# Warming matmuls on a ready-made constant, and the softmax's head masks copied by VectorE

## The chip, the cores and the metric

The kernel runs on one core of a Trainium2 chip. The metric is the device time of one execution in microseconds (us); a lower time is better. Every kernel here was timed in several runs, in turns with the kernel before on the same chip, so each comparison below has its own runs of before.

## The reference, cut to what matters

A causal convolution of 7 taps per head (the taps are a softmax over `weight`), then two matrix products with an ELU between them:

```python
w = softmax(weight, axis=-1)                       # 8 heads x 7 taps
out = einsum('hk,bskhg->bshg', w, unfold(x))       # x: 8 x 4096 x 192, padded by 6 in front
h = out.reshape(32768, 192) @ w_in                 # 192 x 2048
g = where(h > 0, h, exp(minimum(h, 0)) - 1)
return g @ w_out                                   # 2048 x 192, float32
```

## The kernel before: the parts that the change and the argument touch

The work is cut into 32 tiles of 1024 tokens. In the steady state each hidden block of 128 x 512 passes through four engines: TensorE multiplies (line 1029), ScalarE takes the exponential into `E` (760), GpSimd clamps it (714), VectorE makes the product `gT` (871), and TensorE multiplies again (1052). The convolution of all tiles but the first is a matmul with a band matrix `Tm` (1004), which is made from the taps by way of a buffer in DRAM.

The start-up differs: the first tile is loaded by itself (`xs`), cast, transposed on TensorE and convolved tap by tap. Meanwhile GpSimd makes an identity and two masks, and then issues the loads of weights and of the later tiles:

```python
@block.gpsimd
    g.memset(ones[:], 1.0).then_inc(s_id)
    g.affine_select(out=ident[:], in_=ones[:], ...).then_inc(s_id)
    for step in range(2):                          # owner: which head owns which partition
        W(s_id, 2 + step)
        g.affine_select(out=owner[:, :], ...).then_inc(s_id)
    W(s_id, 4)
    g.affine_select(out=block8[:, :, :], ...).then_inc(s_id)
    load_w_in(0); load_w_in(1); load_w_out(0)
    for gr in range(2): load_x(1, gr)
    load_w_out(1); load_w_out(2)
    for gr in range(2): load_x(2, gr)
    for i, (n, u) in enumerate(units):             # the clamps
        ...                                        # (cut: a first load of tile 3 here)
        W(s_exp, i + 1)
        g.tensor_scalar(out=E[...], in0=E[...], scalar1=1.0, scalar2=0.0, op0=min, op1=max)

@block.vector
    v.memset(zw[:], 0.0).then_inc(s_zw)            # operand of the warming matmuls
    v.memset(wband[:], 0.0).then_inc(s_wb)
    v.memset(xbh[:, :, :, :], 0.0).then_inc(s_xz)
    ...                                            # softmax, then (cut)
    W(s_id, 5)
    v.tensor_tensor(wnb[:], block8[:], ..., mult)

@block.tensor
    W(s_zw, 1)
    for _ in range(item[2]):                       # WARM = (6, 1, 4): six, softmax, four
        pe.matmul(H[:, bank, :], zw[:, 0:P], zw[:, 0:GS], start=True, stop=True)
```

## Time and profile before

| | before |
|---|---|
| median of the first three runs | 718.77 us (718.75 to 719.13) |
| span of the profiled run | 716.6 us |
| TensorE, ScalarE, GpSimd, VectorE busy | 99%, 95%, 93%, 90% |
| first hidden matmul, first exponential, first clamp | 10.55, 11.39, 12.86 us |
| start of TensorE's last group (224 matmuls) | 704.35 us |

TensorE bounds the kernel from about 45 us on, and the change alters nothing there. So one asks when the steady state begins. In all lines below, the first number is the start in us from the span's start and the second the length.

### The profile page before, as it was taken

The page shows a single profiled execution, that of the slowest core. Times are in us where ns is not written, and L with a number is a line of the kernel's source. Part 1 is how long each engine was busy: PE and PEld are TensorE (multiplying, and loading weights), DVE is VectorE, ACT ScalarE, POOL GpSimd, SP SyncE. Part 2 cuts the span into 40 slices and gives each one's busy share as a digit, 9 for nine tenths or more (in the row PEclk, how much of TensorE's full clock was granted, in tenths as well). Part 3 has the DMA queues.
Part 4 walks back from the last instruction along what each step waited for, and adds up shares of the span by engine and source line. Part 5 has one row for each costly group of instructions (what it writes and reads, how often), then busy time and mean ns, then how long its engine had stood idle before and what let it go on. Part 6 is the DMA issues. An engine that isn't in the chain of part 4 may idle for free.

```text
span 716.6 us, 27662 instructions
## 1 busy us (share of the span) xinstructions
PE 710.7 (99%) x11873; PEld 681.6 (95%) x11873; DVE 641.5 (90%) x1049; ACT 677.4 (95%) x1290; POOL 663.6 (93%) x1112
## 2 busy tenths in 40 slices
PE   8999999999999999999999999999999999999998
PEld 4699999999999999999999999999999999999998
DVE  7999889998898998899998999988989988999994
ACT  6999999999999999999999999999999999999994
POOL 9999999999999999999999999999999999999893
PEclk9999999999999999999999999999999999999999
DMA  9635334564433544444554344544445534444212
GB/s 183 99 72 95 65 73 78 93 86 76 80 79 74 95 89 64 80 85 79 87 91 69 73 76 95 87 73 76 85 73 91 93 63 78 87 80 83 63 43 69
DMA packets 132303, 58.80 MB, mean 82 GB/s; under 512 B 98374, under 2 KB 131412, under 8 KB 132180
## 3 DMA queue, kind: packets, MB, share of 16 engines
q0 software_dynamic: 43504, 16.77, 22.4%
q1 hardware_dynamic: 88388, 39.37, 22.0%
q8 instruction: 93, 1.52, 0.9%
q10 hardware_dynamic: 288, 0.88, 0.4%
q14 instruction: 30, 0.25, 0.1%
HBM read 34.63 MB, written 25.46 MB: 84 GB/s over the span
## 4 chain that ended last, share of the span: by engine, by line
PE 96%; POOL 2%; ACT 1%; DVE 0%; issue 0%; DVEq 0%; POOLq 0%
PE H L1052 54%; PE H L1029 37%; PE H L1004 4%; POOL xg L631 1%; ACT E L760 1%; POOL E L714 1%; POOL w_in L651 0%; POOL w_out L662 0%; DVE gT L871 0%; ACT csb L756 0%; POOL owner L679 0%; DVE osb L862 0%; POOL block L689 0%; POOL ident L668 0%; POOL ones L666 0%
## 5 line engine op out<-in xcount | busy, mean ns | idle before, releaser
L871 DVE SCALAR_TENSOR_TENSOR gT<-E,H 128x512 f16<-128x512 f32 x1024 | 631.8, 681 | 62.8 <-POOL E L714 58.4
L1029 PE MATMUL H<-att,w_in 64*128 64x512 bf16 x3072 | 679.8, 376 | 1.2 <-DVE gT L871 0.9
L1052 PE MATMUL H<-w_out,gT 64*128 64x192 f16 x8192 | 680.4, 243 | 0.1
L714 POOL TENSOR_SCALAR E<-E 128x512 f32<-128x512 f32 x1024 | 603.0, 611 | 41.1 <-ACT E L760 34.2
L1052 PEld LDWEIGHTS H<-w_out,gT 64*128 64x128 f16 x8192 | 606.7, 94 | 17.5 <-PE H L1052 1.5
L760 ACT ACTIVATE E<-H 128x512 f32<-128x512 f32 x1024 | 585.0, 601 | 23.9 <-PE H L1029 0.4
L1029 PEld LDWEIGHTS H<-att,w_in 64*128 64x128 bf16 x3072 | 275.3, 93 | 7.8 <-DVE gT L871 2.9
L1004 PE MATMUL H<-xg,Tm 64*128 64x240 bf16 x496 | 90.9, 263 | 0.0
L756 ACT ACTIVATE csb<-H 112x480 bf16<-112x480 f32 x124 | 70.7, 570 | 0.4 <-PE H L1004 0.3
L767 ACT ACTIVATE osb<-H 128x384 f32<-128x384 f32 (+1 forms) x129 | 62.0, 482 | 6.9 <-PE H L1052 6.8
L631 POOL DMA_DIRECT2D xg<-in_x_dram x62 | 54.7, 884 | 0.2 <-issue 0.2
L1004 PEld LDWEIGHTS H<-xg,Tm 64*128 64x128 bf16 x496 | 42.6, 94 | 1.2 <-DVE gT L871 0.3
L862 DVE COPY osb<-H 128x192 f32<-128x192 f32 x1 | 0.4, 357 | 7.3 <-PE H L1052 7.3
L909 PE MATMUL H<-zw 128*128 128x512 bf16 x10 | 4.3, 588 | 1.2 <-DVE zw L775 1.2
L909 PEld LDWEIGHTS H<-zw 128*128 128x128 bf16 x10 | 1.2, 134 | 3.0 <-issue 1.7
L651 POOL DMA_DIRECT2D w_in<-in_moe_w_in_dram x6 | 3.6, 612 | 0.0
L736 ACT ACTIVATE xb<-xs 128x512 bf16<-128x512 f32 x2 | 1.2, 622 | 2.4 <-DMA xs<-in_x_dram 2.4
L978 PE MATMUL H<-xT,taps 64*64 64x256 bf16 (+1 forms) x50 | 2.6, 317 | 0.0
L662 POOL DMA_DIRECT2D w_out<-in_moe_w_out_dram x3 | 2.5, 853 | 0.0
L978 PEld LDWEIGHTS H<-xT,taps 64*64 64x64 bf16 x50 | 2.0, 106 | 0.5 <-issue 0.2
L729 ACT ACT_TABLE_LOAD x1 | 1.3, 1283 | 1.2 <-PEq L1119 1.2
L936 PEld LDWEIGHTS H<-ident,xb 64*64 64x64 bf16 x48 | 1.2, 126 | 0.8 <-ACT xb L736 0.8
(45 smaller groups left out, 20.5 us busy)
## 6 DMA issues: line engine op xcount, KB each, us to landing
out_dram<-osb SPq DMA_DIRECT2D x126, 192.0 KB, 2.9
xg<-in_x_dram POOLq DMA_DIRECT2D x61, 240.0 KB, 4.5
xs<-in_x_dram ACTq DMA_DIRECT2D x1, 768.0 KB, 4.6
w_in<-in_moe_w_in_dram POOLq DMA_DIRECT2D x6, 128.0 KB, 4.7
att<-csb SPq DMA_TRANSPOSE x31, 3.9
w_out<-in_moe_w_out_dram POOLq DMA_DIRECT2D x2, 192.0 KB, 7.9
w_out<-in_moe_w_out_dram POOLq DMA_DIRECT2D x1, 384.0 KB, 11.8
w_in<-w_in SPq DMA_DIRECT2D x1, 336.0 KB, 6.8
```

The source lines that it names most:

```text
L631: g.dma_start(xg[0:rows, b, 2 * w0 + gr : 2 * w1 : 2, :], src).then_inc(s_x[b][gr], 16)
L651: g.dma_start(w_in[0:HP, j, c0:c1], bass.AP(tensor=moe_w_in.tensor, offset=8 * j * FF + c0, ap=[[CPH * FF, HEADS], [FF, 8], [1, c1 - c0]], ...
L714: g.tensor_scalar(out=E[:, i % NE, :], in0=E[:, i % NE, :], scalar1=1.0, scalar2=0.0, op0=ALU.min, op1=ALU.max,).then_inc(s_clp)
L756: a.activation(*conv_evac(W, m), ACT.Copy).then_inc(s_ce)
L760: a.activation(E[:, i % NE, :], H[:, bank_of[item], :], ACT.Exp).then_inc(s_exp)
L767: a.activation(*out_evac(W, *item[1:]), ACT.Copy).then_inc(s_oev[item[2]])
L871: v.scalar_tensor_tensor(out=gT[:, s % NG3, q, u, :], in0=E[:, i % NE, :], scalar=1.0, in1=H[:, bank_of[item], :], op0=ALU.subtract, op1=A ...
L909: pe.matmul(H[:, bank, :], zw[:, 0:P], zw[:, 0:GS], start=True, stop=True)
L978: ins = pe.matmul(H[to, bank_of["d", j] + (j == 2 and c0 > 0), c0:c1], taps[rows, tap, rows], xT[rows, j, HALO - PAD + tap + c0 : HALO - P ...
L1004: ins = pe.matmul(H[:, bank_of["c", m], 256 * q : 256 * q + UC], Tm[rows, h, :], xg[rows, s % NXB, :, CPH * h : CPH * (h + 1)].rearrange(" ...
L1029: ins = pe.matmul(H[:, bank_of[item[:3]], :], w_in[HP * r : HP * (r + 1), j, FC * q : FC * (q + 1)], att[HP * r : HP * (r + 1), s % 2, j, ...
L1052: ins = pe.matmul(acc_of(k, g)[:, D * kb : D * (kb + 1)], gT[HP * rt : HP * (rt + 1), t % NG3, q, g, t0 : t0 + P], w_out[HP * rt : HP * (r ...
```

## The change

Its intent is to start the warming of TensorE earlier (it no longer waits for a memset), and to free GpSimd of three selects, so that its loads are issued earlier.

```diff
-WARM = (6, 1, 4)
+WARM = (8, 1, 4)
@@ gpsimd
-            for step in range(2):
-                W(s_id, 2 + step)
-                g.affine_select(out=owner[:, :], ...)
-            W(s_id, 4)
-            g.affine_select(out=block8[:, :, :], ...)
             load_w_in(0)
@@ vector
-            v.memset(zw[:], 0.0).then_inc(s_zw)
             v.memset(wband[:], 0.0).then_inc(s_wb)
             v.memset(xbh[:, :, :, :], 0.0).then_inc(s_xz)
+            W(s_id, 2)
+            v.tensor_copy(owner[:, :]..., ident[0:HEADS, 0:HEADS]...).then_inc(s_own)
+            v.tensor_copy(block8[:, :, :], ident[0:HEADS, 0:HEADS]...).then_inc(s_own)
@@ tensor
-                    W(s_zw, 1)
-                        pe.matmul(H[:, bank, :], zw[:, 0:P], zw[:, 0:GS], ...)
+                        pe.matmul(H[:, bank, :], const 1.0 as (P, P), const 1.0 as (P, GS), ...)
-                    W(s_id, 4)          # ahead of the softmax's matmul
+                    W(s_id, 2)
```

(Cut: the declarations of `zw`, `s_zw`, `s_own`, a wait of the loads on `s_zw`, and VectorE's wait for the masks, now on `s_own`.)

More of the change, by code (lines that the diff above doesn't have):

```diff
@@ L455, in bass_lightweight_conv__then__act_elu_kernel @@
         wband = sbuf("wband", [P, HEADS + 1, BW], BF16)
-        zw = sbuf("zw", [P, GS], BF16)
         scr = sbuf("scr", [P, 2], FP32)
@@ L468, in bass_lightweight_conv__then__act_elu_kernel @@
         s_id = sema("s_id")
+        s_own = sema("s_own")
         s_xs = sema("s_xs")
@@ L480, in bass_lightweight_conv__then__act_elu_kernel @@
         s_z = sema("s_z")
-        s_zw = sema("s_zw")
         s_h = sema("s_h")
@@ L622, in load_x @@
                     W(s_cv, CU * (s - NXB))
-                if s == NXB:
-                    W(s_zw, 1)
                 def windows(w0, w1, rows):
@@ L675, in _gpsimd @@
                 channel_multiplier=1,
-            ).then_inc(s_id)
-            for step in range(2):
-                W(s_id, 2 + step)
-                g.affine_select(
-                    out=owner[:, :],
-                    in_=owner[:, :] if step else ones[0:HEADS, :],
-                    pattern=[[0, 2], [1 - 2 * step, HP]],
-                    compare_op=ALU.is_ge,
-                    fill=0.0,
-                    base=7 * step,
-                    channel_multiplier=8 * (2 * step - 1),
-                ).then_inc(s_id)
-            W(s_id, 4)
-            g.affine_select(
-                out=block8[:, :, :],
-                in_=ones[0:HEADS, 0 : HEADS * KSIZE].rearrange("p (h k) -> p h k", h=HEADS),
-                pattern=[[1, HEADS], [0, KSIZE]],
-                compare_op=ALU.is_equal,
-                fill=0.0,
-                base=0,
-                channel_multiplier=-1,
             ).then_inc(s_id)
@@ L773, in _vector @@
             W = Waits(v)
-            v.memset(zw[:], 0.0).then_inc(s_zw)
             v.memset(wband[:], 0.0).then_inc(s_wb)
             v.memset(xbh[:, :, :, :], 0.0).then_inc(s_xz)
+            W(s_id, 2)
+            v.tensor_copy(
+                owner[:, :].rearrange("p (g h e) -> p g h e", g=2, e=8),
+                ident[0:HEADS, 0:HEADS]
+                .unsqueeze(1)
+                .unsqueeze(3)
+                .to_broadcast([HEADS, 2, HEADS, 8]),
+            ).then_inc(s_own)
+            v.tensor_copy(
+                block8[:, :, :],
+                ident[0:HEADS, 0:HEADS].unsqueeze(2).to_broadcast([HEADS, HEADS, KSIZE]),
+            ).then_inc(s_own)
             W(s_wb, 1)
@@ L800, in _vector @@
             ).then_inc(s_set)
-            W(s_id, 5)
+            W(s_own, 2)
             W(s_set, 5)
@@ L902, in _tensor @@
                 if item[0] == "w":
-                    W(s_zw, 1)
                     bank = bank_of["d", 1]
@@ L908, in _tensor @@
                     for _ in range(item[2]):
-                        pe.matmul(H[:, bank, :], zw[:, 0:P], zw[:, 0:GS], start=True, stop=True)
+                        pe.matmul(
+                            H[:, bank, :],
+                            nc.const_aps.tensor(1.0, (P, P), BF16),
+                            nc.const_aps.tensor(1.0, (P, GS), BF16),
+                            start=True,
+                            stop=True,
+                        )
                 elif item[0] == "s":
-                    W(s_id, 4)
+                    W(s_id, 2)
                     W(s_set, 6)
```

## The prediction

> **What bounds the kernel now.** I read the page's busy shares first, then the chain that ended last, then the first 16 us as a timeline, because the diff touches nothing later.
>
> ```profile
> PE 710.7 (99%) x11873; PEld 681.6 (95%) x11873; DVE 641.5 (90%) x1049; ACT 677.4 (95%) x1290; POOL 663.6 (93%) x1112
> ...
> PE 96%; POOL 2%; ACT 1%; DVE 0%; issue 0%; DVEq 0%; POOLq 0%
> ```
>
> TensorE carries 96% of the chain and bounds everything after about 45 us (in the stretch 45 to 700 it is busy 655.00 of 655.00 us). Its instructions there are unchanged: the instruction order of both builds differs only in the warming group (6 becomes 8), three fewer selects on GpSimd, and one memset traded for two copies on VectorE. So the change can only move the moment at which the steady state begins. The 2% on POOL and the 1% on ACT are that start-up, some 20 us.
>
> The chain in order of time, first 16 us:
>
> ```profile
> 0.79 0.21 POOL ones L666
> ...
> 1.07 0.30 POOL ident L668
> ...
> 1.43 0.30 POOL owner L679
> ...
> 1.79 0.30 POOL owner L679
> ...
> 2.14 0.33 POOL block L689
> 2.48 0.73 POOL w_in L651
> ...
> 10.15 2.69 POOL xg L631 x3
> ...
> 12.86 0.64 POOL E L714
> ```
>
> The columns are start, length, engine and line. GpSimd runs without a gap from the first memset to the first clamp of the ELU at 12.86; its DMA issues stand behind the three selects that the change removes. That makes the selects look like a pure delay of the kernel. But the first clamp also needs the exponential:
>
> ```profile
> 5.44 1.15 ACT L736 ACTIVATE xb<-xs 128x512 bf16<-128x512 f32 x2 [2.39 <-DMA xs<-in_x_dram]
> 5.69 0.56 DVE L819 CAST xb<-xs 128x512 bf16<-128x512 f32 x1
> 6.12 0.86 PE L936 MATMUL H<-ident,xb 64*64 64x64 bf16 x32 [0.21 <-ACT xb L736]
> ...
> 10.55 2.95 PE L1029 MATMUL H<-att,w_in 64*128 64x512 bf16 x23 [0.23 <-DVE att L854]
> ...
> 11.39 3.53 ACT L760 ACTIVATE E<-H 128x512 f32<-128x512 f32 x7
> ```
>
> This is a second chain that the recorded one hides: x tile lands, casts, transposes, the direct convolution of the first tile, first hidden matmul at 10.55, first exponential at 11.39. VectorE has no gap on it between 4.48 and 11.84. It ends at 11.39 + 0.60 = 11.99, so the clamp has at most 12.86 - 12.08 = 0.78 us to gain (0.085 us taken as the hop from ScalarE to GpSimd, the value in the kernel's own schedule model).
>
> **What the Trainium skill says.** "TensorE: Matmul & The Clock Gate", Part 1: the array starts at half clock and goes to full after about 3.4 us of sustained activity, in a free-running window, so the moment varies. The trace agrees: the warming matmuls load weights at 1.65, 2.08, 2.50, 2.93, so 0.43 us apart (512 columns at half clock), the last two of the second group start at 5.2 and 5.5, and the taps matmuls from 7.72 run at full rate. "DMA: Bandwidth & Descriptors", Queues, rings and completion order: each of the 16 engines takes turns between the queues that have work, packet by packet. Before, the two queues hardly meet. The x tile runs on q10, GpSimd's loads on q0:
>
> ```profile
> DMA packets 101, 0.08 MB, mean 158 GB/s; under 512 B 78, under 2 KB 82, under 8 KB 101
> ...
> q0 software_dynamic: 73, 0.02, 45.5%
> q10 hardware_dynamic: 20, 0.06, 27.6%
> ```
>
> This is 4.0 to 4.5 us; from 3.0 to 3.5 the x tile has the engines to itself at 393 GB/s, and q0 has no packet before 4.03 in the packet records. "SBUF — State Buffer", Who interferes with whom: some copies on VectorE hold a port pair that GpSimd needs, for a whole instruction. The trace shows nothing of it here: ident took 0.29 us beside the memset of zw, as did the owner selects beside other memsets.
>
> **The change part by part.**
> 1. GpSimd: two owner selects and the block select go, and the first load is issued after ident. The starts move from 2.43 to about 1.43 - 0.06 = 1.37, so 1.06 us earlier (three steps of 0.36, 0.35 and 0.29 us between starts). The issues themselves last as long as before, so the last x load ends near 11.8 instead of 12.84. The clamp then waits for the exponential and gains at most 0.78 us.
> 2. What of 0.78 reaches the steady state. ScalarE is fully occupied from 11.39 on: between 11.39 and 45 its list of waits has one entry only, 0.44 us at 17.5, for a hidden matmul that waited for a bank, which an earlier clamp and VectorE's product free sooner. After that, at 20.62 to 24.74, the chain runs on ScalarE, and GpSimd waits for ScalarE seven times (1.8 us). So ScalarE started at the same 11.39 caps the gain at about 0.44 us, perhaps 0.5 with smaller gaps.
> 3. VectorE: the 0.27 us memset of zw goes, so that of wband starts at 0.92 instead of 1.26 (0.34 us). The two copies, on 8 partitions, I estimate at 0.2 us each from the small VectorE operations nearby (0.15 to 0.22 us). They start after xbh, at about 1.69, and end at 2.1. The next operation waits until 2.25 for the weights' DMA. Worth zero, and late by 0.1 us at worst, of which the exponential of the taps (2.86, itself behind the table load) hides most.
> 4. TensorE: without the wait for zw, warming starts near 0.9 instead of 1.25. Eight at 0.427 us are 3.4 us: until about 4.3, where six ended at 3.8 and the softmax matmul began at 4.21 on VectorE's word. So that matmul, and the VectorE chain behind it, may start 0.1 us later. The full clock comes perhaps 0.3 us earlier, but the second warming group covers the switch in both kernels and the transposes at 6.12 are already fast: zero.
> 5. The new meeting of queues. GpSimd's loads now reach the DMA engines at 4.03 - 1.06 = 2.97 us, when the x tile (128 packets of 6 KB, 0.234 us each, eight per engine, 1.92 to about 4.1, stragglers to 5.11) is half done. Four to five packets per engine remain. One of GpSimd's packets (0.173 us) between each two would put off the end by up to 4.7 x 0.173 = 0.8 us on an engine that has both. Not all have, and the straggling engine was partly shared already. I take 0.4 us. Of this 0.1 us is slack (the cast on VectorE could begin 0.25 us sooner, the transposed copy at 6.80 about 0.1), so the first exponential is late by 0.3 us.
>
> Sum: -0.45 (part 2) + 0.3 (part 5, which includes the 0.1 of part 4, as both delay the same chain) = **-0.15 us**, so 718.77 - 0.15 = **718.6 us**.
>
> **Rivals.** (a) *The recorded chain is right and nothing takes its place:* about -0.8 to -1.0 us, 717.9. For it: GpSimd stands on the chain for 12 us and every later load lands earlier, too. Against it: the exponential at 11.99 and ScalarE's full queue. (b) *Contention takes it all:* the x tile comes 0.8 us or more later, the whole second chain slides by 0.7, +0.2 to +0.5 us, 719.1. For it: the tile's queue runs at its full rate when the other joins it, and ScalarE waits 2.39 us for it. Against: GpSimd's packets are a third of the size. (c) *A later transfer hides it:* the convolution's band matrix is issued at 13.38 and takes 5.3 us, and the first convolution matmul runs at 19.14, so it has under half a microsecond of room. If the start moves ahead of it, this becomes the wait: zero, 718.8. Against: GpSimd's loads, which share the engines with it, are also through a microsecond earlier. (d) *VectorE's copies or the longer warming delay the softmax:* +0.1 to +0.2 us, visible as a gap before the tap copy longer than 0.41.
>
> **Range and chances.** The rivals span 717.9 to 719.1. The three runs before differ by 0.38 us, and the window of the clock may fall differently. I give 717.6 to 719.6. A move of 2% would be 14 us, and everything that the change touches ends before 16 us: within 2% with 0.985, faster 0.01, slower 0.005.
>
> **What would show it.** Part 1: six issues of w_in from about 1.4 us, the last x load ending near 11.8, and the first clamp no longer back to back with it but waiting for ScalarE. Part 2: the 0.44 us gap of ScalarE near 17.5 gone. Part 4: warming from about 0.9, the softmax matmul at 4.2 to 4.35. Part 5: the first cast on ScalarE at 5.8 instead of 5.44, with both queues in the records between 3 and 4 us, and the first hidden matmul at 10.8 instead of 10.55. If the cast stays at 5.44, part 5 is wrong and the time goes to rival (a), near 718.3. If the first hidden matmul comes at 11.2 or later, rival (b) holds. If the steady state itself takes another time (the stretch 100 to 700 with other rates), the whole argument is wrong.

## The result, and the profile after

The changed kernel took 719.38 us (median of six runs, 718.45 to 720.77), before 718.93 us in its six (718.75 to 719.52). The ratio is 1.0009, with a 95% interval from 0.9996 to 1.0022. A ratio is the mean time of one kernel's runs over that of the other's in the same rounds, so it is not quite the ratio of the medians. The time lies within the range of the prediction. But the forecast was 0.15 us less, and 0.45 us more came, by the medians of the six runs each.

The chain that ended last of the kernel after, first 16 us:

```profile
0.80 4.92 DMA xs<-in_x_dram
...
5.74 0.64 ACT xb L712
...
7.10 0.79 DVE xT L822 x2
...
7.92 0.63 DVE part L829
...
10.14 0.70 DVE att L841
...
10.98 2.88 PE H L1021 x23
```

Before, GpSimd stood here without a gap; now the second chain, which the prediction said lay behind it, is the recorded one. The timelines of GpSimd and ScalarE after show the other side:

```profile
1.45 3.57 POOL L648 DMA_DIRECT2D w_in<-in_moe_w_in_dram  x6
...
9.08 2.66 POOL L628 DMA_DIRECT2D xg<-in_x_dram  x3
12.52 2.35 POOL L690 TENSOR_SCALAR E<-E 128x512 f32<-128x512 f32 x4 [0.78 <-ACT E L736]
...
11.82 3.05 ACT L736 ACTIVATE E<-H 128x512 f32<-128x512 f32 x6 [0.21 <-PE H L1021]
```

GpSimd's loads start 0.98 us earlier and end at 11.74, and GpSimd then waits 0.78 us for the exponential. The first clamp is 0.34 us earlier than before (12.52 against 12.86), although the first exponential is 0.43 us later (11.82 against 11.39).

The end of the chain, before and after, in this order:

```profile
704.35 9.37 PE H L1052 x224
```

```profile
704.27 9.37 PE H L1044 x224
```

In this profile only 0.08 us is left of the 0.34, and the span is 716.7 us against 716.6: nothing gained. To see where it went I compared the start of each of VectorE's 1024 products with that of the same product before: 0.36 us earlier at the first, 0.34 at the 46th, 0.30 at the 101st, then falling slowly to 0.08 at the last. But this run took 718.45 us, and was the fastest of the six. It cannot show what made the others slower.

### The profile page after: what moved, and what is told of

It reads as the page before. It is cut to its first block, busy times and chain, and to the rows that moved or that the text cites. A ratio compares the mean times of both kernels' runs of the same rounds, so it can differ in the third digit from the quotient of the medians.

```text
span 716.7 us, 27664 instructions
## 1 busy us (share of the span) xinstructions
PE 711.2 (99%) x11875; PEld 682.4 (95%) x11875; DVE 642.1 (90%) x1050; ACT 677.3 (95%) x1290; POOL 664.2 (93%) x1109
## 4 chain that ended last, share of the span: by engine, by line
PE 97%; DMA 1%; DVE 1%; POOL 0%; ACT 0%; issue 0%; DVEq 0%
PE H L1044 54%; PE H L1021 38%; PE H L996 4%; DMA xs<-in_x_dram 1%; POOL E L690 0%; DVE part L834 0%; ACT E L736 0%; POOL xg L628 0%; DVE xT L822 0%; DVE att L841 0%; DVE gT L858 0%; PE H L928 0%; ACT xb L712 0%; DVE part L829 0%; ACT csb L732 0%
## 5 line engine op out<-in xcount | busy, mean ns | idle before, releaser
L895 PE MATMUL H<-const-bfloat16-1.0 128*128 128x512 bf16 x12 | 4.6, 544 | 0.8 <-PEq L1111 0.8
```

Source lines behind the costliest of these rows:

```text
L895: pe.matmul(H[:, bank, :], nc.const_aps.tensor(1.0, (P, P), BF16), nc.const_aps.tensor(1.0, (P, GS), BF16), start=True, stop=True,)
```

## The experiments

Twelve further runs were made, in four calls, each call on one chip (e1 and e8 run known kernels once more). A first table for orientation; the columns are explained with the experiments. "Before" is the median of before's runs in the same call. "VectorE" is the number of VectorE's instruction records in the trace, with waits and the final drain. "Fetch" is the start of the last packet of 8192 bytes on queue q14, in the trace's packet records. (Times from the packet records are quoted, here and below, from a zero that lies about 0.09 us ahead of that of the profile's views; within one column this changes nothing.) "Last group" is the start of TensorE's last 224 matmuls, "tail" the time from its end (9.37 us later) to the end of the span.

| kernel | median (range), us | before | VectorE | fetch | last group | tail |
|---|---|---|---|---|---|---|
| before, first profile | | | 1087 | 717.8 | 704.35 | 2.9 |
| after, first profile | 719.38 (718.45 to 720.77) | 718.93 | 1088 | 715.7 | 704.27 | 3.1 |
| e1 after again | 718.98 (718.77 to 719.34) | 718.57 | 1088 | 715.2 | 703.97 | 3.7 |
| e2 warming alone | 718.33 (718.09 to 718.57) | 718.57 | 1086 | 717.9 | 704.35 | 3.0 |
| e3 masks alone | 719.02 (718.54 to 719.34) | 718.57 | 1089 | 714.6 | 704.00 | 3.6 |
| e4 after, six warming | 718.85 (718.42 to 720.31) | 718.57 | 1088 | 716.2 | 704.77 | 2.7 |
| e5 before plus one memset | 719.42 (719.18 to 719.76) | 718.60 | 1088 | 716.3 | 704.75 | 3.9 |
| e6 after minus one | 718.10 (717.95 to 718.43) | 718.60 | 1087 | 717.4 | 704.11 | 2.7 |
| e7 masks alone, two memsets moved | 717.91 (717.83 to 718.09) | 718.60 | 1086 | 717.4 | 703.92 | 2.9 |
| e8 before again, one look | 718.72 | 718.60 | 1087 | 718.0 | 704.42 | 3.1 |
| e9 after, two memsets moved | 718.62 (718.36 to 719.53) | 718.51 | 1085 | 718.4 | 704.41 | 2.9 |
| e10 e7 with idle selects | 718.49 (718.36 to 719.35) | 718.51 | 1086 | 718.0 | 704.46 | 2.9 |
| e11 e7 with two dummies | 718.20 (718.06 to 718.93) | 718.51 | 1088 | 715.3 | 703.98 | 2.9 |
| e12 e7, convolution later | 718.49 (718.28 to 719.56) | 718.72 | 1086 | 718.2 | 704.63 | 3.0 |

Every 95% interval of a ratio holds 1. What carries the argument is the ranges (where they don't overlap) and the profiles.

### First call: is the loss real, and which part makes it

**e1** is the changed kernel unaltered.

> The changed kernel unaltered. Its six runs so far spread over 718.45 to 720.77 us where those of before stay within 718.75 to 719.52; the kept profile is the fastest of them. If the spread belongs to the kernel, five runs here again span 1.5 us or more, with a median of 719.0 to 719.8. If it was chance, they stay within 0.8 us, at 718.3 to 718.8.

Measured: 718.98 us, 0.41 above before. The five runs lie above all nine of before (718.36 to 718.70). So the loss is real. The spread was smaller than forecast, 0.57 us; runs above 719.5 as in the first measurement did not come again here (e4 has two, 719.70 and 720.31). What made the two of the changed kernel (720.76 and 720.77) is not known: no profile of such a run exists.

**e2** is before with the warming part alone, **e3** before with the masks part alone:

```diff
 # e2, against before                       # e3, against before
-WARM = (6, 1, 4)                           -    three selects on GpSimd
+WARM = (8, 1, 4)                           +    two copies on VectorE
-    memset of zw, waits for it
+    constant one as operand
```

> Before with the warming part alone: eight matmuls on the constant one, no memset of zw, masks still by GpSimd. Theory W (the earlier warming is what costs and scatters: the softmax matmul at 4.34 instead of 4.21, or a clock that falls differently): median 0.1 to 0.6 us above before and a spread over 1 us. Theory M (the masks do it, through the earlier GpSimd loads that meet the x tile): within 0.15 us of before, spread as of before, x tile cast by ScalarE at 5.44 as before.

> The masks by VectorE alone: zw, its memset and six warming matmuls as before; GpSimd issues its first load about 1 us earlier. Theory M: the cast of the x tile starts near 5.74 as in the changed kernel, median 0.2 to 0.8 us above before with a spread over 1 us. Theory W: cast at 5.44, first clamp at 12.1 to 12.3, and 0.3 to 0.5 us below before with the spread of before.

Measured: the warming alone 718.33, 0.24 below before (the theory of the masks had forecast within 0.15), with its profile's steady state at the same place as before's (the last group starts at 704.35 in both). The masks alone 719.02, 0.45 above. So the masks make the loss. But the theory that I had given them, a late x tile, fell: its cast starts at 5.45, as before, and the first clamp at 12.09, 0.77 us earlier. The profile of e3 shows its gain arriving and then lost again. The end of its chain, under its span:

```profile
core 0 of [0], span 717.0 us
...
704.00 9.37 PE H L1044 x224
```

TensorE's last group starts 0.35 us before that of the kernel before, yet the span is 0.4 us longer. The loss lies in the last 3.6 us, where nothing is left to do but to store the last results. In e1 it is the same: the group starts at 703.97, the tail is 3.7 us, against 2.9 before.

**e4** is the changed kernel with six warming matmuls on the constant.

> The changed kernel with six warming matmuls instead of eight: the softmax matmul is free of the warming again, at 4.1 to 4.25, so VectorE's chain starts 0.1 to 0.15 us earlier. If the two added matmuls matter: 0.1 us below the changed kernel, more if the spread goes with them. If the x tile's landing sets the chain: no difference from the changed kernel, first hidden matmul still near 10.98.

Measured: 718.85, between the others. The forecast of the softmax's matmul held (4.10). Its profile showed something else. The timeline of TensorE:

```profile
4.10 0.16 PE L905 MATMUL H<-wn,owner 8*128 8x7 bf16 x1 [0.55 <-DVE wnb L790]
4.26 1.89 PE L895 MATMUL H<-const-bfloat16-1.0 128*128 128x512 bf16 x4
6.16 1.47 PE L928 MATMUL H<-ident,xb 64*64 64x64 bf16 x32
```

After six early matmuls TensorE sits idle for 0.55 us, and the 32 transposes take 1.47 us instead of 0.86, as they would at a low clock (this profile has no record of the clock). With eight, in e1, the pause is gone and the transposes take 0.86. So the two added matmuls belong to the constant: they fill the time that the earlier start opens. The first exponential of this run came at 12.61, 1.2 us later than before, and still the last group starts only 0.42 us later. The steady state absorbs two thirds of a loss of the start-up, as it does of a gain.

### What happens in the last three microseconds

In the packet records of the end I looked for what differs between before and e2 (tail 2.9 to 3.0 us) and e1 and e3 (3.6 to 3.7). Fifteen of the 16 parts of the last store complete together; in e1 and e3 the last part is 0.67 us later. At the same time there is one packet of 8192 bytes on q14, which the profile calls "instruction", of 616 and 709 ns, where before and e2 have it only after the end of the span. In e1 the data of the last part begin at 715.70 in the views' time, just when the fetch ends. (The records do not name the DMA engine; that the two share one is read from these times.) The DMA views of 714 to 717.2 us, first before:

```profile
GB/s 374 365 384 356 365 365 279 96 0 221 365 355 250 96 240 374 355 356 384 346 269 77 0 0 0 0 0 0 0 0 0 0 0 0 0 0 0 0 0 0
...
q1 hardware_dynamic: 589, 0.40, 38.0%
q10 hardware_dynamic: 144, 0.10, 9.2%
```

The columns of the GB/s line are 40 slices of 0.08 us. q1 and q10 carry the stores; after 715.8 there is nothing, and no line of q14. What sets such a fetch off? The change alters instruction counts on three engines. VectorE's is the one that fits: 1086 or 1087 records where the fetch comes after the end, 1088 or 1089 where it comes into the stores.

This was the theory of the second call (T), and its rival was that the loss is made in the start-up alone (S). **e5** is before with one instruction more on VectorE, put where it idles; **e6** the changed kernel with one fewer:

```diff
 # e5, against before
+            v.memset(pad1[:, :], 0.0)      # 128 x 1, ahead of the first product
             for item in dve_order:
 # e6, against after
-            v.memset(xbh[:, :, :, :], 0.0).then_inc(s_xz)      # VectorE
+            a.memzero(xbh[:, :, :, :]).then_inc(s_xz)          # ScalarE, idle there
```

> Before with one dummy memset (one column) on VectorE, in its idle 1.7 us ahead of the first product: 1088 recorded VectorE instructions instead of 1087, nothing else. Theory T (the last 8 KB fetch of instructions belongs to VectorE's stream and is set off at its 1088th instruction; in the masks kernels it then lands in the drain of the last output): the 8 KB packet moves from 717.8 to between 714.5 and 716.5, the start-up is as before (first exponential 11.4, clamp 12.86), and the median is 0.2 to 0.9 us above before with a wider spread. Rival S (the loss is made in the start-up alone): the packet stays near 717.8 and the time within 0.15 us of before.

> The changed kernel with the memset of xbh moved from VectorE to ScalarE (idle there): 1087 VectorE instructions as in before. Theory T: the 8 KB packet is back near 717.5, the time from the end of TensorE to the end falls from 3.1 to 3.7 to about 2.9 us, and the median is 0.2 to 0.4 us below before, 0.5 to 0.8 below the changed kernel. Rival S: the packet's place does not follow, and the median stays 0.4 above before.

Measured: e5 719.42, 0.82 above before, all five runs (719.18 and more) above all nine of before (up to 718.80). e6 718.10, 0.50 below before. The fetch moved as forecast, to 716.3 in e5 and to 717.4 in e6. The same view of e5:

```profile
GB/s 173 336 384 355 394 336 384 375 355 384 173 39 77 288 384 307 164 10 96 336 365 384 365 365 327 183 39 102 0 0 0 0 0 0 0 0 0 0 0 0
...
q1 hardware_dynamic: 704, 0.49, 46.1%
q10 hardware_dynamic: 144, 0.10, 9.2%
q14 instruction: 1, 0.01, 1.4%
```

The q14 line is there now, and the stores run until 716.2. The last column with anything in it is the fetch, from 716.28 (716.20 in the views' time). Here the data of the last part are written just before it, and what stands behind it, at 717.03, is the semaphore write that completes the store (the packet records; 4 bytes are too little for the GB/s line). Tail 3.9 us. In fairness: in the profile of e5 TensorE's last group is also 0.4 us late, so only 1.0 of the 1.4 us between its span of 718.0 and before's 716.6 is the tail. Most of the 0.4 comes at one point: VectorE's first 14 products are 0.06 us ahead of before's and the 15th is 0.30 behind, because the band matrix lands at 19.38 us instead of 18.70. Its way through DRAM had begun at 6.86, as before, and the added memset ran only at 13.29; why it took longer is not known. That the kernel with a single memset of one column more, in an idle stretch, takes 0.8 us longer is shown by the five runs; how much of it is the tail is known for the profiled one alone.

**e7** is the masks-only kernel with two memsets moved to ScalarE:

```diff
-            v.memset(wband[:], 0.0).then_inc(s_wb)
-            v.memset(xbh[:, :, :, :], 0.0).then_inc(s_xz)
+            a.memzero(xbh[:, :, :, :]).then_inc(s_xz)          # ScalarE, behind the softmax's exponential
+            a.memzero(wband[:, :, :]).then_inc(s_wb)
```

(VectorE's wait for `wband` moves down to the first use of it.)

> The masks part alone (zw and six warming matmuls as before) with the memsets of xbh and of wband moved to ScalarE: 1086 to 1087 VectorE instructions. Theory T: packet near 717.5, first clamp 12.1 as in the masks-only run, TensorE's last group starts near 704.0 instead of 704.35, and the median is 0.3 to 0.5 us below before. Rival S: 0.4 above before like the masks-only run.

> Before, unaltered, for a second profile: how far the start-up moves by itself. Cast of the x tile within 0.3 us of 5.44, first exponential 11.2 to 11.6, TensorE's last group at 704.35 within 0.15, 8 KB packet after 717.

Measured: e7 717.91, 0.69 below before, all five runs (at most 718.09) below all nine of before (at least 718.27). It is the fastest of the kernels run on this chip; the changed kernel was not among them. Before (e8) held in every point: cast at 5.46, exponential at 11.47, last group at 704.42, fetch at 718.0. The tail of e7, in the same view and window:

```profile
GB/s 365 326 164 19 115 326 336 336 183 288 384 326 394 365 384 212 39 0 0 0 0 0 0 0 0 0 0 0 0 0 0 0 0 0 0 0 0 0 0 0
...
q1 hardware_dynamic: 397, 0.27, 25.2%
q10 hardware_dynamic: 144, 0.10, 9.2%
```

The stores end 0.4 us earlier than before's, and no fetch is among them.

Over all fourteen profiles the split has no exception: up to 1087 records the fetch starts at 717.4 or later, from 1088 on between 714.6 and 716.3, whatever GpSimd's count (1119 or 1122) and whichever warming. Whether it costs anything is a matter of order. In e1, e3 and e5 a part of the last store stands behind it (tails of 3.6 to 3.9); in the profiled runs of after, e4 and e11 it comes just behind (2.7 to 3.1). So the changed kernel's fastest run, whose profile was kept, was a lucky one.

### Third call: what the early loads are worth, and the fetch once more

**e10** is e7 with three idle selects on GpSimd, so that its loads start late again; **e11** is e7 with two dummy memsets on VectorE; **e9** is the whole changed kernel with e7's move.

```diff
 # e10, against e7: GpSimd, ahead of load_w_in
+            for step in range(3):
+                g.affine_select(out=idle[:, :], ...).then_inc(s_idle)
 # e11, against e7: VectorE, ahead of the first product
+            for i in range(2):
+                v.memset(pad1[:, i : i + 1], 0.0)
```

> The masks-only version with both memsets on ScalarE, and with three dummy selects on GpSimd in the place of the removed ones, so that its loads start at 2.43 us again. If the gain comes from the earlier loads: first clamp back at 12.86, TensorE's last group at 704.35, median within 0.2 us of before. If it comes from the shorter VectorE stream or the moved memsets: median 0.4 to 0.7 us below before all the same.

> The masks-only version with both memsets on ScalarE, plus two dummy memsets on VectorE in its idle stretch ahead of the first product: 1088 VectorE instructions, start-up as without them. Theory T: clamp at 12.0 and TensorE's last group near 703.95 as without them, the 8 KB packet between 714.3 and 716.3, and the median 0.4 to 0.9 us above the version without them (with it in the same call: above 718.2). If the packet alone costs nothing: 717.8 to 718.0.

> The changed kernel (eight warming matmuls on the constant one) with the memsets of xbh and wband moved to ScalarE: 1085 VectorE instructions. Beside the masks-only version with the same moves (717.91 on another chip), it tells what the other warming is worth when the end is clean. If nothing: 717.8 to 718.1, about 0.5 to 0.7 below before. If the earlier VectorE start counts: 717.7 or less. If the longer first group hurts: over 718.2.

Measured: e10 718.49, before 718.51. With the loads back at 2.43 us the gain is gone (last group at 704.46). So the gain of e7 is that of the earlier loads, as the prediction had it. e11 has a median of 718.20, just at the forecast's bound, but its runs fall into two groups: 718.06, 718.11, 718.20 and 718.90, 718.93. The profile is of the first group, and its fetch (715.29) starts just ahead of the end of the stores (715.32). Two groups 0.7 us apart are what a race between the fetch and the last store would give; that the second group lost it is argued, as only one profile was kept.

e9 missed: 718.62 instead of 717.8 to 718.1. Its tail is clean (fetch at 718.4), but its profile has the late start-up (exponential at 11.82), and its products slip from 0.24 us ahead of before's (the 21st) to 0.05 behind (the last). The profile of after slips in the same way, e1 and e11 do not. The cause of this slip, 0.3 us over 650, stays open. So does the question whether the constant one is worth anything when the end is clean: e6 and e9, which have it, stand at -0.50 and +0.11 on two chips.

### Why the start-up comes early or late, and what caps its gain

The profiles fall into two kinds: the first hidden matmul at 10.45 to 10.63 us (before, e2, e3, e6, e7, e8, e10) or at 10.96 to 11.21 (after, e1, e5, e9, e11, e12); e4 with its slow transposes is apart. Of the kernels with early loads five of eight are late, of those with late loads one of five (e5); whether the early loads make a late start likelier, so few profiles cannot tell. The late ones share one line. VectorE's first tap product, in before and then in e12, where its chain had begun at the same time:

```profile
7.61 0.49 DVE L842 TENSOR_SCALAR part<-xT,wcol 128x512 f32<-128x512 bf16 x1
```

```profile
7.63 0.88 DVE L834 TENSOR_SCALAR part<-xT,wcol 128x512 f32<-128x512 bf16 x1
```

It takes 0.49 us in all the early profiles but one (e10, 0.70, begun at 7.44), and 0.56 to 0.95 in the late ones. In after, e1, e9, e11 and e12 it starts anywhere from 7.63 to 7.97 and always ends at 8.51 to 8.54: it is held until a fixed moment. GpSimd is issuing loads at that time, but so it is in the early profiles (before: a load from 7.59 to 8.51, beside the 0.49 us above). This may be the case that the Trainium skill describes ("SBUF — State Buffer", Who interferes with whom): a `tensor_scalar` on VectorE can take a port pair that it shares with GpSimd, and the second to come waits. The five equal ends are measured; that the ports do it is not shown, and why the same product is not held in before or e3 (begun at 7.61 and 7.62) is open.

**e12** asked what caps the gain. In e3, e6 and e7 the first clamp comes 0.77 to 0.88 us earlier than before, and the 16th product only 0.31 to 0.39. The gain drops in one step, at the 15th product (in e3 from 0.79 to 0.35). The waits of TensorE from 14 to 22 us, before and in e3, name what takes the rest:

```profile
PE H L1029 <- DVE gT L871: 0.8, 1, 0.8
```

```profile
PE H L996 <- DMA Tm<-conv_band: 0.2, 1, 0.2
```

That is rival (c) of the prediction: the band matrix lands at about 18.7 us, and the first convolution matmul, wanted earlier now, waits for it: in e3, e6 and e7 it starts 0.05 us after the landing. In e12 the first convolutions are asked for one step later:

```diff
-EARLY_CONV = (7, 8, 9, 10)
+EARLY_CONV = (8, 9, 10, 11)
```

> The masks-only version with both memsets on ScalarE (0.7 us below before on its chip), and the first four convolution units each one step later, so that TensorE asks for the band matrix about 1.2 us later. Rival (c) of the prediction (the band matrix's landing is what cut the clamp's gain from 0.78 to 0.89 down to 0.31 to 0.40 us between products 10 and 15): TensorE no longer waits for the band's DMA, product 20 on VectorE comes 0.6 to 0.9 us earlier than in before, and the median is 1.0 to 1.2 us below before. ScalarE's cap (part 2): the wait for the band goes but product 20 stays within 0.3 to 0.5 us of before's place, and the median 0.5 to 0.8 us below before.

Measured: 718.49, 0.23 below before: a miss. The wait for the band is gone, and the 21st product comes 0.70 us earlier than before's although this run has a late start-up (exponential at 11.80). Part of that lead is the move itself, which the forecast had not reckoned with: by then before has made four of ScalarE's copies for the convolution (0.57 us each), e12 three. Where the counts are equal again, from the 28th to the 32nd product, the lead is 0.40, and the products ahead of the first convolution had 0.38; so e12 doesn't separate the two theories. And the next tile's convolution is then finished too late, and another wait takes the place, in TensorE's list of waits from 11 to 45 us:

```profile
PE H L1021 <- DVE att L846: 0.6, 1, 0.6
PE H L1021 <- DMA att<-csb: 0.4, 1, 0.4
```

Behind the second, the transposed tile, the 36th product is 0.21 us later than before's. So the early steps stand between two transfers, the band matrix ahead and the transposed tile behind: in the traces the gain of the start-up is cut to about 0.4 us at the one (e3, e6, e7) or lost at the other (e12).

## Why the prediction was right, and where it was wrong

The range held the time, and "within 2%" was never in doubt. But the range was 2 us wide, and the median of every kernel of this record lies in it (717.91 to 719.42), so that this speaks for no mechanism. The forecast had the wrong sign. By its own steps:

1. **GpSimd's part was right.** The loads start at 1.45 (forecast 1.37), end at 11.74 (11.8), and the clamp waits for ScalarE, as said.
2. **"What of 0.78 reaches the steady state": the size was right, the cause in part another.** Forecast 0.45 us; 0.35 (e3), 0.24 (e6) and 0.43 (e7) reach TensorE's last group. I took ScalarE's full queue for the cap. In e3, e6 and e7 it is the band matrix, which I had listed as rival (c) and set aside. ScalarE's gap near 17.5 did go, as forecast. But in e1 and e11 ScalarE begins at 11.80 and 11.81, 0.41 us later than before, and still TensorE's last group is 0.38 and 0.37 us earlier: the start of ScalarE doesn't set the cap. Nor was it full: the prediction counted its one listed wait, but by the windows it was busy for 5.43 of the 6 us from 14 to 20 and for 24.47 of the 25 from 20 to 45, so short gaps hold 0.66 us more.
3. **VectorE's copies cost what was estimated** (0.15 and 0.17 us, ended by 1.9), hidden in front of the weights' DMA. But I counted their time alone, and not that they are instructions.
4. **The warming was right**: from 0.83, the softmax matmul at 4.34 in the first profile (forecast 4.2 to 4.35). (The timeline has the six of before end at 3.99, not at 3.8 as I had worked out.) What I did not see is why there are eight: six leave a pause and slow transposes (e4).
5. **"The new meeting of queues" failed in its mechanism.** The cast did come at 5.74 in the first profile, close to the forecast 5.8, so at first it looked confirmed. But GpSimd's first packet is at 4.03 us (3.95 in the views' time), as before, although issued 0.98 us earlier, and from 4.0 to 4.5 us the queues of after carry numbers of packets close to those that the prediction shows of before (73 and 20), GpSimd's with a larger share:

```profile
q0 software_dynamic: 77, 0.03, 77.5%
q10 hardware_dynamic: 16, 0.06, 27.3%
```

   There is no earlier meeting with the x tile. In all fourteen profiles, with the loads issued at 1.45 or at 2.43, GpSimd's first packet comes 0.01 to 0.15 us after the first of the x tile's 16 completions, that is, when the first engine is through with its share. The page that I cited ("DMA: Bandwidth & Descriptors", Queues, rings and completion order) says that an engine drains a packet of some 9 to 17 descriptors before it switches. An engine's share of the x tile is eight rows and one semaphore write, so nine; it may be one packet. I had taken each record of the trace for a packet. And in e3, e6 and e7 the cast starts at 5.34 to 5.45, with the same early loads, so they don't always make it late. Whether they do so at times stays open: the cast starts at 5.57 to 5.80 in four of the nine profiles with early loads, and by 5.46 in all five with late ones. The packets account for little of it: the x tile's last completion is written at 5.03 us before, at 5.17 after and at 5.05 in e9, which has the latest cast (views' time).
6. **The step that made the sum wrong** is one sentence under "Range and chances": "everything that the change touches ends before 16 us". The change makes VectorE's stream one instruction longer, and with that the last fetch of instructions falls among the last stores. Worth up to 0.7 to 1.0 us a run, it turns a forecast of -0.15 into +0.4. Without it (e6, one memset moved to ScalarE) the change gives -0.50 on its chip.

The rivals: (a), nothing takes the place, came closest in e7 (717.91, forecast 717.9), though for a kernel other than the one forecast and partly by luck: on its own chip that is -0.69, against a forecast of -0.8 to -1.0. (b), contention, gives the right sign by a wrong mechanism. (c) is real, as a cap. (d) is not seen.

## What to carry to other kernels

When a change of the start-up moves the time less than, or against, what the start-up's profile says, compare the last group of the bounding engine and the tail behind it, before looking for more at the front: here (e1, e3) the front had gained 0.35 to 0.38 us and the tail lost 0.7 to 0.8. The number of instructions of an engine can matter by itself when a fetch of them falls into the final store, so test with a dummy instruction in an idle stretch, one more and one fewer. And one profile is one run: the kept profile of the changed kernel was its luckiest, and showed nothing of the loss.

## What the Trainium skill lacked or had wrong

- "DMA: Bandwidth & Descriptors", Queues, rings and completion order, names row 14 as runtime-internal with its refills, but not that such a fetch can hold up a kernel's last store. The runs show one packet of 8192 bytes on q14, of 0.62 to 0.74 us, ahead of the last part of a store, and tails of 3.6 to 3.9 us instead of 2.7 to 3.1. "Runtime: NRT & Kernel Launch", Instruction fetch mechanics, gives refills in blocks of 256 instructions and calls the cost of a boundary mostly hidden; no page says how to tell from a trace where the last one falls. Here it was between 1087 and 1088 records of VectorE, and it was not hidden (e5: +0.82 us with one instruction more).
- The same section is right on packets where a reader of trace records may go wrong: GpSimd's loads, issued at 2.43 (before) or at 1.45 us (after), both have their first packet at 4.03 us, just behind the first engine's completion of its share of the x tile, eight rows and a semaphore write.
- "TensorE: Matmul & The Clock Gate", Part 1, gives the switch to full clock as about 4 us into activity, give or take 0.5 us from run to run. The clock records of twelve of these profiles have it at 3.82 to 6.47 us (views' time), with the first matmul at 0.83 or 1.25, so 3.0 to 5.2 us in, with short pauses of the activity near 4 us; two profiles have no record of it, and in one of these (e4) the transposes at 6.16 still ran slowly (1.47 us instead of 0.86).
- "SBUF — State Buffer", Who interferes with whom, would fit what is seen of VectorE's first tap product (up to 0.95 us instead of 0.49, its end at 8.51 to 8.54 in five profiles), but GpSimd issues loads beside the short ones too, so these runs don't show it; the prediction's sentence that the trace shows nothing of it spoke only of the masks and the memsets.
